# A new instruction order for the first stage of a three-part kernel, and a last output copied by two engines

## The chip, the cores and the metric

The kernel runs on one core of one Trainium2 chip. The metric is device time in microseconds (us) of one execution. The core's engines each run their own instruction stream in order: TensorE does matmuls (PE in the rows), VectorE is DVE, ScalarE is ACT, GpSimd is POOL, and SyncE (SP) issues nearly all DMA transfers.

## The reference, cut to what matters

Three computations follow each other; all of it is in float32.

```python
# attention: q, k, v, f_logit are (4, 8, 768, 48)
f = 1 / (1 + exp(-f_logit))
for t in range(768):
    state = f[:, :, t, :, None] * state + einsum('bhd,bhe->bhde', k[:, :, t], v[:, :, t])
    y[:, :, t] = einsum('bhd,bhde->bhe', q[:, :, t], state)
x = y as (4, 768, 384)
# first block
theta = x @ w_theta                                   # 384 x 384
u = x + w_tok_r @ (x * cos(theta)) + w_tok_i @ (x * sin(theta))   # 768 x 768 each, per batch
x = u + relu(u @ w_ch)                                # 384 x 384
# second block
h = relu(x @ w_in); u, v = h[..., :512], h[..., 512:]
v_n = (v - mean(v)) / sqrt(var(v) + 1e-6)
v_s = w_spatial @ v_n + b_spatial                     # 768 x 768, per batch
out = (u * v_s) @ w_out                               # 512 x 384
```

## The kernel before, in words

**Two stages.** Stage 1 computes attention and the first block for all four batches and prepares the weights of the second block. It ends some 357 to 365 us into the span, the engines not all at the same time. Stage 2 does the second block, one batch after the other, and fills the rest.

**Exact products.** A float32 operand is split into a high and a low part; a product of two split operands is three matmuls. So a row of a group such as `pv` x9 is one output tile: three slices of the contraction, three matmuls each.

**Names in stage 1.** `k`, `q`, `f`, `cw`, `icp`, `cu`, `fs` and `qp` belong to attention: `pt` are transposes of k, `psc` the scores (masked by DVE into `sc`), `pw` the sums of the state (scanned by DVE into `cu`), `px` the attention output, which lands in `X`. `pth` is theta. `acc` is token mixing: `tk` is a slice of the mixing weights, brought by DMA, and `z` is x times cosine or sine. DVE's `xt<-acc,xt` adds the mixing result to x, `uT<-xt,uT` makes its low part, and `hh<-uT,wc` is the product with `w_ch`. DVE's `xt<-hh,xt` adds the relu of that and so frees the PSUM bank of `hh`. `x2d<-xt` stores the result to DRAM. Between these stand the weights of stage 2: `ws`, `wb`, `wi`, `wo` (loaded, split, kept in SBUF) and `X`, `wt`, `wz` with stores `wpd`, which turn `w_spatial` (loaded by `X<-wp_dram` into the buffer `X0` that held a batch of x before) into the blocks of a seven-product scheme.

**Names in stage 2.** Per batch: `pv` (6 tiles of 9 matmuls, 128x512), whose relu ACT writes to `vr`; DVE takes its statistics (`st`, `mv`, small `l` chains, of which ACT does two steps) and normalises it; `pu` (8 tiles of 9); `vn` are the seven operands made from the normalised v by ACT (high part) and DVE (low part); `pg` are seven products of 18 matmuls (P1, P2, P6, P7, P4, P5, P3 in that order) with `sp`, the blocks of `w_spatial` loaded back from DRAM; DVE combines and gates them (`g`, `gt`); `po` (6 tiles of 12) is the product with `w_out`, which ACT copies to `oo` and SP stores to `out_dram`. P1 needs the first three of the six normalised tiles, P2 the other three.

**What sets the order.** In stage 1 it is written out. Every operation is recorded by `Plan` (so all rows carry line L258, the helper's); the operations of a matmul group form one unit, every other operation is a unit of its own, and the table `LINE` (line 65 on) lists the units of each engine in the order in which the engine must run them: "T" TensorE, "V" VectorE, "A" ScalarE, "G" GpSimd, "Q" SyncE. `Plan.run` (lines 233 to 258) chains each engine's instructions accordingly. In stage 2 the tile scheduler orders the instructions by itself, from the order in which `p2_v`, `p2_b`, `p2_u`, `p2_f`, `p2_o` ask for them and from when it thinks operands are there.

**Around the boundary.** Stage 2's PSUM pool has eight buffers on the same eight banks that stage 1 used, so a `pv` tile can start only when the last reader of the bank's old content is done. `flag` (line 1021) runs at the start of stage 2: DVE reduces `ge` to `gt` and `gr`, SP moves `gr` to one partition (`gc<-gr`), DVE sums it (`gs<-gc`), and the result decides at the very end, in a branch (line 1270), whether a general fallback runs. With these inputs it does not run.

**The start.** `run(...)` puts FILL = 16 matmuls of an identity matrix by itself (`pt<-ident`) into the stream. Their result is not used; they keep TensorE busy while the first operands are made.

**The outputs.** `p2_o` (lines 1009 to 1018) takes a tile `oo` from a pool with two buffers, has ACT copy the PSUM tile into it and has SP store it.

## Time and profile before

| | us |
|---|---|
| median of 3 runs | 611.06 |
| lowest, highest | 609.41, 612.85 |
| the profiled execution, its own time | 613.34 |
| span of its trace, first to last instruction | 611.6 |
| TensorE matmul busy | 580.7 (95%) |
| VectorE busy | 454.0 (74%) |
| ScalarE busy | 355.4 (58%) |
| GpSimd busy | 31.9 (5%) |
| mean granted TensorE clock, as a share of full speed | 0.979 |

The profiled execution is 2.28 us longer than the median, and 1.7 us of its time lie outside the span. Times in the trace count from the start of the span. TensorE is busy nearly all the time, so what matters are the few places where it is not, and the few where its granted clock is at the lower of its two levels. How such a row is read: a line of the timeline gives start, duration, engine, operation, output <- inputs, how many instructions are drawn together, and in brackets the idle time of that engine just before and what ended it.

### The profile page before, as it was taken

The numbers are of one execution on the slowest core, as the hardware profiler recorded it, in microseconds if no ns is written. First come the engines' busy times: TensorE is split into PE (matmuls) and PEld (weight loads), VectorE is DVE, ScalarE is ACT, GpSimd is POOL, SyncE is SP. The second block draws the span as 40 slices with busy tenths as digits, with TensorE's granted clock in tenths as the row PEclk, the third lists the DMA queues.
The fourth block names the chain that finished last, engine by engine and source line by source line (L and its number), as shares of the span: only waits on it lengthen the run. The fifth ranks groups of instructions, "written<-read, shape, count | busy, mean of one in ns | idle before, by whom it ended". The sixth has DMA issues, their size and how long they took to land. (4 is left out here: it accounts for less than half of the span.)

```text
span 611.6 us, 14051 instructions
## 1 busy us (share of the span) xinstructions
PE 580.7 (95%) x5686; PEld 532.2 (87%) x5686; DVE 454.0 (74%) x815; ACT 355.4 (58%) x683; POOL 31.9 (5%) x95
## 2 busy tenths in 40 slices
PE   5699999999999999999999959999999999999994
PEld 5676667867989999999999948999999999999994
DVE  4988999888886587776768684896669576948680
ACT  5778897679784798656753252634443444335321
POOL 4410101000110010100000000000000000000000
PEclk9789999999999999999999998999999999999998
DMA  7669768679877897678788979496029504930511
GB/s 238 190 216 332 240 235 276 211 222 308 283 278 277 267 315 254 219 255 266 248 315 309 350 267 302 138 376 243 27 94 379 211 13 140 374 132 1 182 70 65
DMA packets 68442, 139.45 MB, mean 228 GB/s; under 512 B 6480, under 2 KB 40656, under 8 KB 68368
## 3 DMA queue, kind: packets, MB, share of 16 engines
q1 hardware_dynamic: 68368, 138.46, 66.6%
q8 instruction: 47, 0.77, 0.5%
q14 instruction: 27, 0.22, 0.1%
HBM read 104.20 MB, written 31.85 MB: 222 GB/s over the span
## 5 line engine op out<-in xcount | busy, mean ns | idle before, releaser
L258 PE MATMUL acc<-tk,z 128*128 128x384 f32 x792 | 172.2, 367 | 0.4 <-DMA tk<-tkp 0.4
L258 PEld LDWEIGHTS acc<-tk,z 128*128 128x128 f32 x792 | 138.3, 188 | 16.5 <-DMA tk<-tkp 0.7
L258 PE MATMUL pg<-sp,vn 128*128 128x384 f32 x504 | 88.0, 336 | 0.0
L258 PEld LDWEIGHTS pg<-sp,vn 128*128 128x128 f32 x504 | 87.4, 188 | 0.0
L258 PE MATMUL pv<-wi,x 128*128 128x512 f32 x216 | 53.5, 406 | 5.8 <-DVE xt L258 5.8
L258 PEld LDWEIGHTS pv<-wi,x 128*128 128x128 f32 x216 | 42.4, 197 | 15.0 <-DVE xt L258 6.2
L258 PE MATMUL po<-wo,gt 128*128 128x384 f32 x288 | 51.8, 338 | 0.0
L258 PEld LDWEIGHTS po<-wo,gt 128*128 128x128 f32 x288 | 50.8, 188 | 0.3
L258 PE MATMUL pu<-x,wi 128*128 128x384 f32 x288 | 50.7, 334 | 0.0
L258 PEld LDWEIGHTS pu<-x,wi 128*128 128x128 f32 x288 | 50.1, 188 | 0.3
L258 PE MATMUL hh<-uT,wc 128*128 128x384 f32 x216 | 41.7, 342 | 1.1 <-ACT uT L258 0.7
L258 PEld LDWEIGHTS hh<-uT,wc 128*128 128x128 f32 x216 | 37.9, 188 | 2.4 <-ACT uT L258 1.0
L258 ACT ACTIVATE gt<-g 128x384 fp32r<-128x384 f32 x32 | 16.7, 522 | 37.5 <-DVE g L258 37.3
L258 DVE BATCH_NORM_STATS2 st<-vr 128x6 f32<-128x512 f32 x24 | 16.6, 691 | 27.2 <-ACT vr L258 27.1
L258 DVE TENSOR_TENSOR vn<-vr,vn 128x768 fp32r<-128x768 f32 x24 | 22.9, 955 | 18.6 <-ACT vn L258 17.9
L258 ACT ACTIVATE vn<-vr 128x768 fp32r<-128x768 f32 x24 | 20.3, 845 | 20.0 <-PE pg L258 17.9
L258 PE MATMUL pth<-wh,xT 128*128 128x384 f32 x108 | 31.7, 348 | 0.0
L258 PE MATMUL px<-vc,sc 64*64 64x48 f32 x768 | 28.0, 225 | 0.0
L258 ACT ACTIVATE sn<-sn 128x384 f32<-128x384 f32 x48 | 24.9, 520 | 5.1 <-DVE sn L258 4.7
L258 ACT ACTIVATE oo<-po 128x384 f32<-128x384 f32 x24 | 11.8, 492 | 26.1 <-PE po L258 21.3
L258 PEld LDWEIGHTS px<-vc,sc 64*64 64x64 f32 x768 | 25.5, 144 | 0.1
L258 ACT ACTIVATE ws<-ws 128x768 f32<-128x768 f32 (+2 forms) x28 | 20.6, 737 | 6.8 <-DMA ws<-wi_dram 3.3
(138 smaller groups left out, 1053.8 us busy)
## 6 DMA issues: line engine op xcount, KB each, us to landing
sp<-wpd SPq DMA_DIRECT2D x56, 576.0 KB, 6.5
tk<-tkp SPq DMA_DIRECT2D x48, 384.0 KB, 4.9
ws<-tok_dram SPq DMA_DIRECT2D x12, 768.0 KB, 6.0
tkp<-tk SPq DMA_DIRECT2D x24, 384.0 KB, 6.5
tkd<-tk SPq DMA_DIRECT2D x12, 384.0 KB, 5.7
x2d<-xt SPq DMA_DIRECT2D x24, 192.0 KB, 3.8
ws<-tkd SPq DMA_DIRECT2D x12, 384.0 KB, 5.0
xs<-x2d SPq DMA_DIRECT2D x12, 384.0 KB, 6.6
```

Source lines behind the costliest of these rows:

```text
L258: r = f(*a, **k)
```

## The change

All five rows of `LINE` are replaced: the same units on the same engines, in another order. `p2_o` gets a third buffer for `oo` in all batches, and for the very last output tile the PSUM tile is copied in two halves, left by ACT and right by DVE, each stored by a DMA of its own, the left issued by SP and the right by ACT.

```diff
 LINE = {
     "T": [
-        45, 61, 46, 47, 82, 48, 49, 50, 51, 52, 53, 54, 55, 56, 57, 58, 59, 60, 95, 91, 100, 120, 131, 127, 142, 136, 146, 151, 160, 156, 165, 185,
+        45, 61, 46, 47, 48, 49, 50, 51, 52, 53, 54, 55, 56, 57, 58, 59, 60, 82, 91, 95, 100, 120, 127, 131, 136, 142, 146, 151, 156, 160, 165, 185,
...
-    def p2_o(self, out):
+    def p2_o(self, out, last=False):
         gt, wo = self.gt, self.wo
         for t in range(NT):
             sl = slice(P * t, P * t + P)
             p = self.p2.tile([P, FF], F32, name="po", tag="mm")[:, 0:DM]
             self.mm3(p, [(gt[0][:, f, sl], gt[1][:, f, sl], wo[0][:, f], wo[1][:, f]) for f in range(NF)])
-            o = self.d2.tile([P, DM], F32, name="oo", tag="oo")
-            self.A.activation(o, p, AF.Copy)
-            self.Q.dma_start(out=out[sl, :], in_=o)
+            o = self.d2.tile([P, DM], F32, name="oo", tag="oo", bufs=3)
+            if last and t == NT - 1:
+                lo, hi = slice(0, DM // 2), slice(DM // 2, DM)
+                self.A.activation(o[:, lo], p[:, lo], AF.Copy)
+                self.V.tensor_copy(o[:, hi], p[:, hi])
+                self.Q.dma_start(out=out[sl, lo], in_=o[:, lo])
+                self.A.dma_start(out=out[sl, hi], in_=o[:, hi])
+            else:
+                self.A.activation(o, p, AF.Copy)
+                self.Q.dma_start(out=out[sl, :], in_=o)
             yield
...
-            run(self.p2_o(a["out"][b]))
+            run(self.p2_o(a["out"][b], b == B - 1))
```

What the table does shows in the instruction streams. Three places follow; a row is one instruction, or several alike with their count, and a number behind a name tells buffers and operations apart.

VectorE, the last instructions of stage 1, before; `hh_4718` and `hh_4734` are the last two `hh` tiles:

```order
L258 TENSOR_TENSOR X0_134<-X0_134,wz_4698 128x768
L258 TENSOR_SCALAR wb_4820<-ws_4821 128x384
L258 SCALAR_TENSOR_TENSOR wb_4820<-ws_4821,wb_4820 128x384 x2
L258 TENSOR_TENSOR X0_134<-X0_134 128x768
L258 TENSOR_TENSOR wo1_4349<-wb_4820,wo0_4348 128x384
L258 TENSOR_TENSOR wt_4699<-wt_4699,wz_4698 128x384
L258 TENSOR_SCALAR wb_4829<-ws_4830 128x384
L258 TENSOR_TENSOR wt_4699<-wt_4699,X0_134 128x768
L258 SCALAR_TENSOR_TENSOR xt_4067<-hh_4718,xt_4067 128x384
L258 SCALAR_TENSOR_TENSOR wb_4829<-ws_4830,wb_4829 128x384 x2
L258 TENSOR_TENSOR wo1_4349<-wb_4829,wo0_4348 128x384
L258 SCALAR_TENSOR_TENSOR xt_4067<-hh_4734,xt_4067 128x384
```

The reader of `hh_4718` stood behind eight rows of weight work, and that of `hh_4734`, stage 1's last row on this engine, behind two more. The same place in the changed kernel:

```order
L258 TENSOR_TENSOR wo1_4349<-wb_4811,wo0_4348 128x384
L258 TENSOR_SCALAR wb_4820<-ws_4821 128x384
L258 SCALAR_TENSOR_TENSOR xt_4067<-hh_4718,xt_4067 128x384
L258 SCALAR_TENSOR_TENSOR xt_4067<-hh_4734,xt_4067 128x384
L258 SCALAR_TENSOR_TENSOR wb_4820<-ws_4821,wb_4820 128x384 x2
L258 TENSOR_TENSOR X0_134<-X0_134 128x768
L258 TENSOR_TENSOR wo1_4349<-wb_4820,wo0_4348 128x384
L258 TENSOR_TENSOR wt_4699<-X0_134,wt_4699 128x384
L258 TENSOR_TENSOR X0_134<-X0_134,wz_4698 128x768
L258 TENSOR_TENSOR wt_4699<-wt_4699,X0_134 128x768
L258 TENSOR_SCALAR wb_4829<-ws_4830 128x384
L258 SCALAR_TENSOR_TENSOR wb_4829<-ws_4830,wb_4829 128x384 x2
```

The last two readers of `hh` have moved ahead of most of the weight work; nine rows of it now stand behind them before stage 1 ends on this engine (the seven shown and two more, for `wt` and `wo1`).

VectorE, a little earlier, where the last three `acc` tiles are read, before:

```order
L258 TENSOR_TENSOR xt_4067<-acc_4486,xt_4067 128x384
L258 TENSOR_TENSOR uT1_4673<-xt_4067,uT0_4672 128x384
L258 SCALAR_TENSOR_TENSOR xt_3917<-hh_4528,xt_3917 128x384
L258 TENSOR_TENSOR xt_4067<-acc_4488,xt_4067 128x384
L258 TENSOR_TENSOR xt_4067<-acc_4487,xt_4067 128x384
L258 TENSOR_TENSOR uT1_4673<-xt_4067,uT0_4672 128x384 x2
L258 TENSOR_TENSOR wt_4699<-X0_134 128x384
L258 TENSOR_TENSOR X0_134<-X0_134 128x384
```

and in the changed kernel:

```order
L258 TENSOR_TENSOR xt_4067<-acc_4486,xt_4067 128x384
L258 TENSOR_TENSOR wt_4699<-X0_134 128x384
L258 TENSOR_TENSOR X0_134<-X0_134 128x384
L258 TENSOR_TENSOR uT1_4673<-xt_4067,uT0_4672 128x384
L258 TENSOR_TENSOR xt_4067<-acc_4488,xt_4067 128x384
L258 TENSOR_TENSOR xt_4067<-acc_4487,xt_4067 128x384
L258 TENSOR_TENSOR uT1_4673<-xt_4067,uT0_4672 128x384 x2
```

The two operations that read the last load of `w_spatial` into `X0` have moved ahead of the second and third `acc` reader. On SP that load's two transfers stand four and seven rows earlier than before, each still behind the stores that read the buffer's old content.

TensorE at the very start, before; `k0_137` and `k1_203` are the k of the first two attention units:

```order
L258 MATMUL pt_178<-ident_60 128x128
L258 MATMUL pt_195<-ident_60,k0_137 128x128 x3
L258 MATMUL pt_178<-ident_60 128x128 x2
L258 MATMUL pt_223<-ident_60,k1_203 128x128 x3
L258 MATMUL pt_178<-ident_60 128x128 x13
L258 MATMUL pw_252<-vn0_100,kt_110 64x48
```

and in the changed kernel:

```order
L258 MATMUL pt_178<-ident_60 128x128
L258 MATMUL pt_195<-ident_60,k0_137 128x128 x3
L258 MATMUL pt_178<-ident_60 128x128 x15
L258 MATMUL pt_223<-ident_60,k1_203 128x128 x3
L258 MATMUL psc_235<-qp0_105,k0_137 64x64 x12
L258 MATMUL pw_252<-vn0_100,kt_110 64x48
```

Fifteen fillers stand together now, ahead of the second unit's transposes instead of around them, and the first scores stand ahead of the first state sums.

## Rows read from the trace of the kernel before

**Rows 1.** Windows: length, busy us per engine, PEclk, DMA share, GB/s.

```profile
core 0: us, PE busy (x) PEld busy (x) DVE busy (x) ACT busy (x) POOL busy (x), PEclk, DMA share, GB/s
20.00:40.00 20.00, 15.89 (x378) 14.18 (x377) 17.54 (x34) 14.86 (x42) 6.42 (x22) 0.68 0.66 214
140.00:160.00 20.00, 20.00 (x190) 17.83 (x189) 18.63 (x27) 16.94 (x30) 1.21 (x4) 1.00 0.98 340
360.00:380.00 20.00, 15.27 (x57) 12.71 (x58) 9.44 (x30) 5.90 (x13) 0.00 (x0) 0.83 0.86 277
```

**Rows 2.** Chain that ended last, in time order: start, us, what.

```profile
364.74 13.32 PE pv L258 x45
...
390.57 21.84 PE pg L258 x126
...
429.22 8.20 PE pv L258 x36
```

**Rows 3.** Timeline, all engines, end of stage 1.

```profile
356.75 2.24 PE L258 MATMUL pv<-wi,x 128*128 128x512 f32 x9
...
361.46 0.55 DVE L258 SCALAR_TENSOR_TENSOR xt<-hh,xt 128x384 f32<-128x384 f32 x1
...
362.03 2.99 SPq L258 DMA_DIRECT2D x2d<-xt  x3
363.10 0.52 ACT L258 ACTIVATE wo<-wb 128x384 fp32r<-128x384 f32 x1 [2.55 <-DVE wb L258]
...
364.13 0.55 DVE L258 SCALAR_TENSOR_TENSOR xt<-hh,xt 128x384 f32<-128x384 f32 x1
...
364.74 13.32 PE L258 MATMUL pv<-wi,x 128*128 128x512 f32 x45 [5.75 <-DVE xt L258]
```

**Rows 4.** Windows around two pauses of TensorE.

```profile
181.00:184.00 3.00, 1.70 (x38) 1.33 (x36) 1.30 (x2) 2.85 (x5) 0.00 (x0) 1.00 1.02 374
...
364.00:371.00 7.00, 6.26 (x15) 4.96 (x16) 3.18 (x11) 2.61 (x5) 0.00 (x0) 0.52 0.69 195
```

**Rows 5.** Timeline, the flag and the operands of the first products.

```profile
369.63 0.61 SPq L258 DMA_DIRECT2D gc<-gr  x1
...
376.39 0.27 DVE L258 TENSOR_REDUCE gs<-gc 1x1 f32<-1x128 f32 x1 [8.14 <-DMA gc<-gr]
376.59 0.67 DVE L258 BATCH_NORM_STATS2 st<-vr 128x6 f32<-128x512 f32 x1
...
383.37 0.93 DVE L258 TENSOR_TENSOR vn<-vr,vn 128x768 fp32r<-128x768 f32 x1
...
388.60 0.96 DVE L258 TENSOR_TENSOR vn<-vr,vn 128x768 fp32r<-128x768 f32 x1
```

**Rows 6.** Timeline, the last load of `w_spatial` and the last `acc` readers.

```profile
345.65 0.81 SPq L258 DMA_DIRECT2D X<-wp_dram  x2
...
347.19 0.56 DVE L258 TENSOR_TENSOR xt<-acc,xt 128x384 f32<-128x384 f32 x1 [1.45 <-PE acc L258]
...
352.91 0.56 DVE L258 TENSOR_TENSOR wt<-X 128x384 f32<-128x384 f32 x1 [0.88 <-DMA X<-wp_dram]
```

**Rows 7.** Timeline, the fillers and the first scores.

```profile
6.44 0.90 PE L258 MATMUL pt<-ident,k 128*128 128x128 f32 x3 [3.47 <-DVE k L258]
...
10.02 4.19 PE L258 MATMUL pt<-ident 128*128 128x128 f32 x26
...
14.52 0.88 PE L258 MATMUL psc<-qp,k 64*64 64x64 f32 x24
...
15.52 0.56 DVE L258 TENSOR_TENSOR sc<-psc,mask 128x384 f32<-128x384 f32 x1 [3.18 <-PE psc L258]
```

**Rows 8.** Timeline, the last outputs.

```profile
598.75 4.39 PE L258 MATMUL po<-wo,gt 128*128 128x384 f32 x24
...
601.27 3.49 SPq L258 DMA_DIRECT2D out_dram<-oo  x3
...
603.92 0.49 ACT L258 ACTIVATE oo<-po 128x384 f32<-128x384 f32 x1 [1.43 <-DMA out_dram<-oo]
```

122 rows, old and new, of the table LINE are left out of this document.

## The prediction

> **What bounds the kernel now.** I read the share of busy time first: TensorE's matmuls are busy 95% of the span, so time is won only where TensorE waits, where it runs at its lower clock, or behind its last matmul. The 20 us windows then show where that is. From 44 to 340 us every window is full; [rows 1] shows one of the fullest for all engines, 140 to 160, with VectorE at 18.63 of 20. Two places are not full. From 20 to 40 TensorE is busy 15.89 at a mean clock of 0.68, and from 360 to 380 it is busy 15.27 at 0.83 [rows 1].
>
> The chain that ended last gives the second place its parts [rows 2]: `pv` 13.32 us, `pu` up to 390.57, `pg` 21.84. The timeline shows what lies ahead [rows 3]: the first `pv` tile starts at 356.75 and ends at 358.99, then TensorE stands still for 5.75 us until 364.74, and the row names VectorE's `xt`. That is the reader of the last `hh` tile, at 364.13, which frees a PSUM bank; the reader before it runs at 361.46. Their own inputs did not hold them: TensorE runs in order, so the matmuls of `hh` were over about when `pv` began at 356.75. VectorE was working through weights.
>
> The pause has a second price. In the window behind it the granted clock is 0.52, that is the lower level (1.2 of 2.4 GHz) for nearly all of it [rows 4]. The 45 `pv` matmuls took 13.32 us; the next batch's 36 took 8.20, 0.228 each, by which 45 take 10.25 [rows 2]. So 3.07 us went to the clock. A shorter pause did not do that: TensorE is busy only 1.70 of 3.00 us from 181 to 184, around a pause of 1.3, and the clock stays 1.00 [rows 4].
>
> **The change part by part.** *End of stage 1.* The two last readers of `hh` now stand ahead of nine rows of weight work. VectorE can run them as soon as `hh` is done, some 357.5 us, ahead of 358.99 when the second `pv` tile wants its bank. So TensorE goes on at 358.99, without the pause and the lower clock: `pv` ends at 358.99 + 10.25 = 369.24, `pu` (390.57 - 378.06 = 12.51) at 381.75. If nothing else were late, `pg` would start 8.82 us earlier, and all of stage 2 behind it. ScalarE does not spoil this: its last work of stage 1 still waits for VectorE's weights to about 363.6 [rows 3], but the pool has eight buffers for six `pv` tiles, so its copies are wanted only when the third `pu` tile comes, after 372.
>
> What is late next is the operands of `pg`. VectorE needs the normalised `v`, and in its stream stands the flag's sum `gs`, which waits for a transfer: issued at 369.63, there at 376.39, VectorE idle 8.14 us for it [rows 5]. Behind it, P2's operand `vn` ends at 388.60 + 0.96 = 389.56, 13.17 after `gs` began. The changed kernel has four BN_STATS ahead of `gs` where before had one: 3 x 0.67 = 2.0 less behind it. The first tile's small chain and normalising now stand behind it: one tile of the five that took the 13.17, so at most 2. I take 12.5 (11.2 to 13.2). The transfer itself is behind the stores on SP. Before, the three stores of the last `xt` held SP 2.99 us until 365.0 [rows 3]; now these go out some 6 us earlier, but the last stores of weights still wait for VectorE, whose total work is the same. I take the flag as landing 2.0 earlier, at 374.4, between no gain (376.4) and the 2.4 that the rest of the 2.99 could give. Then P2's operand is there at 386.9. Its products and all behind, 108 of 126 matmuls, take 18.72, so `pg` ends at 405.6 instead of 412.41: **6.8 us gained**. Bounds: with the flag as before and 13.2 behind it, P2 is ready at 389.6 and the gain is 4.1; with nothing late it is 8.8. P1's operand (383.37 before, 5.2 us ahead of P2's) comes at about 382, so TensorE waits twice for about a microsecond; by the pause of 1.3 in [rows 4] I let the clock stay up.
>
> By the Trainium skill (TensorE: Matmul & The Clock Gate, "What's actually happening") the throttled state is the default and activity releases it; the 0.52 behind the 5.75 us pause agrees. The 1.00 around the pause of 1.3 agrees too, and what the rule would make of two pauses close together is the first rival.
>
> *Start.* Before, the first scores `psc` stood behind 13 fillers (26 records, 10.02 to 14.21) and began at 14.52, and VectorE idled 3.18 us for them [rows 7]. Now 15 fillers follow directly on the first unit's transposes (which begin at 6.44); at 0.32 each they end at about 12, then three transposes of 0.5 in sum, and `psc` may begin at 12.4, about 2.1 earlier. VectorE's own row, added up to the first `z` product with the traced durations, is 2.3 shorter. These are the same gain seen from two engines, so I take **2.0** for the whole start. How much of it arrives at 44 us is uncertain, since TensorE's clock is at the lower level in a third of this stretch (0.68, [rows 1]): bounds -2 (the clock falls in other places) and +5 (psc, VectorE's row and a better clock all count).
>
> *Middle, 44 to 340 us.* TensorE is full and the same matmuls run: 0. Moved weight and store work is covered by TensorE's own work; that cover is thinnest at 140 to 160, where VectorE is at 18.63 of 20. Bounds -4 and +1.
>
> *Tail.* The last `oo` copy waited for a buffer, 1.43 us after the one before and until the store issued at 601.27 had landed [rows 8]; the last matmul ends at 598.75 + 4.39 = 603.14. With three buffers it starts about 0.7 earlier than 603.92, and half a tile takes about half of 0.49: **0.9** (0.5 to 1.0). That the halves go out on two engines saves one issue on SP at most; the span ends 611.6, long behind either.
>
> The Trainium skill (DMA: Bandwidth & Descriptors, "Issuing engines are not separate DMA queues") says that issuing from two engines saves only the issuing time, which speaks against a gain from the split store. No row here has one. The sum does without it: it rests on the copy.
>
> *Sum.* 6.8 + 2.0 + 0 + 0.9 = 9.7. The profiled execution goes from 613.34 to 603.6; it lies 2.28 above the median, and the same difference on 611.06 gives **601.4**. Own range: with end and start both at their good bounds it would be 5.0 less, at their bad ones 6.7 more; two thirds of these give 598.1 to 605.9.
>
> **The rivals.** *The flag takes most of it back.* If the flag lands as before, the gain there is 4.1. TensorE then waits about 1.5 for P1 and 2 for P2; if that lowers the clock, another 3.07 goes. 4.1 - 3.07 = 1.0, and 1.0 + 2.0 + 0.9 = 3.9, so 607.2. For it: the last weight stores ahead of the flag wait for the same VectorE work as before. Against it: P1's 18 matmuls lie between the two pauses.
>
> *A new wait on a load, and the kernel is slower.* VectorE now reads the last load of `w_spatial` ahead of the second and third `acc` readers. It gets there at 347.19 + 0.56 = 347.75. Before, the load was issued at 345.65 and used only at 352.91, after waiting 0.88 for it [rows 6]. Each microsecond that it lands after 347.75 holds up `uT`, `hh` and stage 2, and beyond about 2 the clock's 3.07 comes on top. Landing at 352.9 as before costs 5.2 + 3.07 = 8.3, so 609.7 and almost nothing gained. It decides against the change from 354.3 on (9.7 - 3.07 = 6.6 past 347.75), and by 358 the kernel is at 614.7. For it: the load's buffer must first be stored, and the store waits for VectorE. Against it: the transfers stand four and seven rows earlier on SP; at 345.65 less about 0.5 us a row they go at 342 to 343 and land by 349, a loss of about one us that the third `acc` reader, which waits for TensorE anyway, mostly hides.
>
> *VectorE becomes the bound in the middle, or the start gains nothing.* VectorE's work ahead of the `acc` reader near 144 us grows by 2.7 by the same adding up, against a slack of 1.37 in the window [rows 1]. If that and a start of 0 come together, 6.8 + 0.9 - 1.3 to -4 = 3.7 to 6.4: 604.7 to 607.4, about 606.
>
> *The order does not do what it says.* If another reader still holds the second `pv` tile's bank, only the start and the tail remain: 2.9, 608.2.
>
> **How the numbers follow.** Forecast 0.56 (598.1 to 605.9); better than that 0.06; flag 0.13 (607.2); load 0.10, of which half beyond 354.3; middle or start 0.11 (606); no release 0.04 (608.2). A measurement of this kernel can tell about 0.5%, 3.06 us, from no change: faster means below 608.0, slower above 614.1. Faster: 0.56 + 0.06 + 0.12 of the flag + 0.01 of the load + 0.10 of the middle + 0.01 = 0.86. Same 0.10, most of it the load between 350 and 354 and past it a little. Slower 0.04. The range leaves out the load's worse half, the best tenth of the start and the cases without release: 596.5 to 608.5.
>
> **What would show it.** Right: no pause between the first `pv` tile and the next over 0.3 us, a clock of 1.00 from 356 to 380, `pv` over by 367 to 371 (the start's gain included), `pg` over by about 404, and `psc` beginning at 12 to 13. Wrong: VectorE idle ahead of `wt<-X` with a DMA as releaser near 348; `gs` later than 375; a clock below 1 in 380 to 390; TensorE waiting for VectorE between 130 and 150; or the last `oo` copy still released by a DMA.

## The result, and the profile after

| | before | after |
|---|---|---|
| median, both kernels measured on the same chip, us | 611.95 | 601.82 |
| lowest, highest | 609.41, 614.19 | 599.95, 603.56 |
| ratio, 95% interval | | 0.984 (0.980 to 0.987) |
| the profiled execution, its own time | 613.34 | 599.95 |
| span of its trace | 611.6 | 598.2 |

The changed kernel is faster by 10.1 us; 601.4 was forecast. The two profiled executions differ by more, 13.4 us: that of before lies 1.4 above its median, that of after is the fastest of its kernel, 1.9 below its median. Pieces read from these two traces therefore add up to 13.4, and not to 10.1.

Windows of the kernel after, with the columns of [rows 1] (stretch, length, busy us of each engine, granted clock, DMA share, GB/s), the three stretches shown there and three more:

```profile
20.00:40.00 20.00, 16.90 (x395) 14.71 (x386) 17.01 (x35) 15.14 (x41) 6.36 (x22) 0.74 0.73 236
...
140.00:160.00 20.00, 20.00 (x227) 18.21 (x227) 18.96 (x27) 17.53 (x28) 1.41 (x5) 1.00 0.97 352
360.00:380.00 20.00, 20.00 (x111) 19.18 (x110) 14.73 (x52) 12.32 (x30) 0.00 (x0) 1.00 0.94 307
380.00:400.00 20.00, 20.00 (x117) 20.00 (x116) 18.58 (x32) 8.48 (x13) 0.00 (x0) 1.00 0.94 325
400.00:420.00 20.00, 18.20 (x96) 16.78 (x95) 11.14 (x27) 6.91 (x15) 0.00 (x0) 1.00 0.57 208
...
180.00:200.00 20.00, 20.00 (x365) 18.97 (x363) 14.72 (x22) 14.55 (x26) 1.55 (x5) 1.00 0.93 330
```

From 360 to 380 TensorE is busy all 20 us at a clock of 1.00, where it had 15.27 at 0.83 [rows 1]. The start is a little fuller (16.90 for 15.89, clock 0.74 for 0.68). A new gap stands from 400 to 420: 18.20. And from 180 to 200 TensorE is full, where before had 18.70 at a clock of 1.00.

The end of stage 1, timeline of all engines, which answers [rows 3] and [rows 6]:

```profile
343.65 0.55 DVE L258 TENSOR_TENSOR wt<-X 128x384 f32<-128x384 f32 x1
...
351.93 1.20 DVE L258 SCALAR_TENSOR_TENSOR xt<-hh,xt 128x384 f32<-128x384 f32 x2
352.38 12.44 PE L258 MATMUL pv<-wi,x 128*128 128x512 f32 x54
```

All 54 `pv` matmuls run in one piece; the two readers of `hh` end at 353.13, before the second tile wants its bank (354.45). The read of the last load of `w_spatial` at 343.65 waits for nothing. The rest of [rows 2] in the chain of waits of after (start, us, what):

```profile
352.54 12.28 PE pv L258 x54
364.82 12.51 PE pu L258 x72
...
417.55 8.65 PE pv L258 x38
```

The flag and the operands, which answer [rows 5], all engines:

```profile
362.75 0.62 SPq L258 DMA_DIRECT2D gc<-gr  x1
...
368.86 0.27 DVE L258 TENSOR_REDUCE gs<-gc 1x1 f32<-1x128 f32 x1 [1.65 <-DMA gc<-gr]
...
374.44 0.95 DVE L258 TENSOR_TENSOR vn<-vr,vn 128x768 fp32r<-128x768 f32 x1
377.16 22.00 PE L258 MATMUL pg<-sp,vn 128*128 128x384 f32 x126
378.62 0.96 DVE L258 TENSOR_TENSOR vn<-vr,vn 128x768 fp32r<-128x768 f32 x1
```

`pg` waits for no operand at all: P1's is there at 375.4, P2's at 379.58, and P2 begins about 380.3, after P1's 18 matmuls. What came late instead lies further on, ahead of the fourth `po` tile of the first batch. A tile's twelve matmuls come in two groups of six, and this is the seventh group, as it is called below:

```profile
391.26 0.33 SPq L258 DMA_DIRECT2D xs<-x2d  x1
...
397.62 0.85 ACT L258 ACTIVATE x<-xs 128x768 fp32r<-128x768 f32 x1 [6.70 <-DMA xs<-x2d]
398.38 0.93 ACT L258 ACTIVATE gt<-g 128x384 fp32r<-128x384 f32 x2
...
407.30 1.32 PE L258 MATMUL po<-wo,gt 128*128 128x384 f32 x6 [1.80 <-ACT gt L258]
```

The start and the last outputs, which answer [rows 7] and [rows 8]:

```profile
7.00 5.03 PE L258 MATMUL pt<-ident 128*128 128x128 f32 x30
...
12.29 0.86 PE L258 MATMUL psc<-qp,k 64*64 64x64 f32 x22
...
13.25 0.56 DVE L258 TENSOR_TENSOR sc<-psc,mask 128x384 f32<-128x384 f32 x1 [1.28 <-PE psc L258]
```

```profile
592.03 0.33 ACT L258 ACTIVATE oo<-po 128x192 f32<-128x192 f32 x1 [0.74 <-PE po L258]
592.39 0.36 DVE L258 COPY oo<-po 128x192 f32<-128x192 f32 x1 [7.11 <-ACT oo L258]
```

The last copy no longer waits for a store; but VectorE's half runs behind ScalarE's, not beside it.

Two tables, worked out from the matmul records, carry what follows. First landmarks (us; the start of the matmul, if nothing else is said), each row one profiled execution:

| kernel | last `acc` | first `pv` | second `pv` tile | first `pu` | second batch's `pu` | last matmul ends | span |
|---|---|---|---|---|---|---|---|
| before | 349.94 | 356.75 | 364.74 | 377.90 | 437.26 | 603.14 | 611.6 |
| after | 345.92 | 352.38 | 354.45 | 364.65 | 426.04 | 591.95 | 598.2 |
| e1_table | 344.45 | 350.92 | 352.98 | 363.18 | 424.51 | 590.89 | 598.1 |
| e2_out | 351.18 | 357.46 | 365.13 | 378.14 | 437.50 | 603.40 | 611.7 |
| e4_readers | 349.29 | 355.57 | 357.63 | 367.83 | 427.50 | 593.40 | 601.8 |
| e3_behind | 346.30 | 352.76 | 360.72 | 372.97 | 432.33 | 598.32 | 604.4 |
| e9_bank | 351.39 | 359.29 | 361.35 | 371.55 | 436.79 | 602.70 | 611.5 |
| h1_start | 350.52 | 357.31 | 362.63 | 374.58 | 434.66 | 600.73 | 607.4 |
| h2_end | 359.88 | 366.35 | 368.43 | 378.63 | 439.51 | 605.42 | 612.5 |
| e8_fill | 347.98 | 355.22 | 363.29 | 375.57 | 434.93 | 600.84 | 609.9 |
| e10_xlast | 345.54 | 352.00 | 354.08 | 364.28 | 427.22 | 593.61 | 600.0 |
| e11_xsoon | 345.91 | 352.37 | 354.43 | 364.63 | 425.22 | 591.12 | 597.3 |

Second, when TensorE had the same work behind it. At the six places of this table all five kernels have started the same number of matmuls of every kind, so that times in one row can be compared; each is the start of the next matmul (us).

| matmuls started | before | e2_out | e8_fill | after | e1_table |
|---|---|---|---|---|---|
| 786 | 54.16 | 54.16 | 51.80 | 50.34 | 49.05 |
| 1396 | 95.48 | 95.66 | 94.00 | 91.88 | 90.57 |
| 1579 | 101.69 | 101.87 | 100.26 | 99.29 | 98.39 |
| 2391 | 178.89 | 179.26 | 177.38 | 176.99 | 175.51 |
| 2696 | 190.28 | 192.19 | 188.96 | 186.85 | 185.38 |
| 4258 | 331.80 | 333.04 | 329.84 | 327.77 | 326.31 |

before and e2_out run the old table, after and e1_table the new one, so the two pairs (before and after, e2_out and e1_table) say how far a difference repeats. before and e2_out run stage 1 alike and still lie 1.9 us apart after 2,696 matmuls; a difference of that size between two single executions need not be one between their kernels.

### The profile page after: what moved, and what is told of

It reads as the page before. It is cut to its first block, busy times and chain, and to the rows that moved or that the text cites. A ratio compares the mean times of both kernels' runs of the same rounds, so it can differ in the third digit from the quotient of the medians.

```text
span 598.2 us, 14051 instructions
## 1 busy us (share of the span) xinstructions
PE 575.8 (96%) x5686; PEld 529.2 (88%) x5686; DVE 452.7 (76%) x816; ACT 355.4 (59%) x683; POOL 30.7 (5%) x95
## 4 chain that ended last, share of the span: by engine, by line
PE 89%; DVE 4%; DMA 2%; ACT 1%; issue 1%; DVEq 0%; ACTq 0%
PE acc L258 27%; PE pg L258 11%; PE pu L258 8%; PE pv L258 8%; PE po L258 7%; PE pth L258 7%; PE hh L258 6%; PE px L258 4%; PE psc L258 4%; PE pt L258 3%; PE pw L258 3%; DVE g L258 1%; DMA xs<-x2d 1%; DMA ws<-tok_dram 1%; DVE vn L258 1%
## 5 line engine op out<-in xcount | busy, mean ns | idle before, releaser
L258 PE MATMUL acc<-tk,z 128*128 128x384 f32 x792 | 171.2, 368 | 0.0
L258 PEld LDWEIGHTS acc<-tk,z 128*128 128x128 f32 x792 | 138.7, 189 | 16.2 <-issue 0.5
L258 PE MATMUL pg<-sp,vn 128*128 128x384 f32 x504 | 88.0, 336 | 0.0
L258 PEld LDWEIGHTS pg<-sp,vn 128*128 128x128 f32 x504 | 87.4, 188 | 0.0
L258 PE MATMUL po<-wo,gt 128*128 128x384 f32 x288 | 52.1, 338 | 1.8 <-ACT gt L258 1.8
L258 PEld LDWEIGHTS po<-wo,gt 128*128 128x128 f32 x288 | 50.8, 188 | 2.4 <-ACT gt L258 2.1
L258 PE MATMUL pu<-x,wi 128*128 128x384 f32 x288 | 50.7, 335 | 0.0
L258 PEld LDWEIGHTS pu<-x,wi 128*128 128x128 f32 x288 | 50.1, 188 | 0.3
L258 PE MATMUL pv<-wi,x 128*128 128x512 f32 x216 | 50.4, 390 | 0.0
L258 PEld LDWEIGHTS pv<-wi,x 128*128 128x128 f32 x216 | 40.5, 188 | 8.1
L258 PE MATMUL hh<-uT,wc 128*128 128x384 f32 x216 | 42.0, 343 | 0.8 <-ACT uT L258 0.7
L258 PEld LDWEIGHTS hh<-uT,wc 128*128 128x128 f32 x216 | 37.7, 188 | 1.9 <-ACT uT L258 1.0
L258 DVE BATCH_NORM_STATS2 st<-vr 128x6 f32<-128x512 f32 x24 | 16.5, 690 | 26.5 <-ACT vr L258 26.5
L258 DVE TENSOR_TENSOR vn<-vr,vn 128x768 fp32r<-128x768 f32 x24 | 22.9, 954 | 17.3 <-ACT vn L258 16.5
L258 ACT ACTIVATE gt<-g 128x384 fp32r<-128x384 f32 x32 | 16.5, 521 | 32.0 <-DVE g L258 31.9
L258 PE MATMUL pth<-wh,xT 128*128 128x384 f32 x108 | 32.1, 351 | 0.0
L258 ACT ACTIVATE vn<-vr 128x768 fp32r<-128x768 f32 x24 | 20.3, 844 | 18.2 <-PE pg L258 17.3
L258 PE MATMUL px<-vc,sc 64*64 64x48 f32 x768 | 27.8, 223 | 0.0
L258 ACT ACTIVATE ws<-ws 128x768 f32<-128x768 f32 (+2 forms) x28 | 20.4, 732 | 11.0 <-DMA ws<-wo_dram 5.1
L258 ACT ACTIVATE u<-pu 128x384 f32<-128x384 f32 x32 | 15.7, 490 | 18.5 <-PE pu L258 18.5
L258 ACT ACTIVATE sn<-sn 128x384 f32<-128x384 f32 x48 | 24.9, 520 | 2.2 <-DVE sn L258 1.7
L258 PEld LDWEIGHTS px<-vc,sc 64*64 64x64 f32 x768 | 25.4, 143 | 0.0
```

Source lines behind the costliest of these rows:

```text
L258: r = f(*a, **k)
```

## The experiments

Each ratio is to the kernel before, measured beside it. Where a table takes more lines, the helper's rows carry L265 instead of L258.

**e1_table and e2_out: the two halves of the change apart.** e1_table has the new table and `p2_o` of before; e2_out the old table and the new `p2_o`.

```diff
 e1_table, against after
-            o = self.d2.tile([P, DM], F32, name="oo", tag="oo", bufs=3)
-            if last and t == NT - 1:
...
+            o = self.d2.tile([P, DM], F32, name="oo", tag="oo")
+            self.A.activation(o, p, AF.Copy)
+            self.Q.dma_start(out=out[sl, :], in_=o)
```

> The new order table with the old outputs (two buffers, last tile in one piece). Theory: the table carries nearly everything; the outputs are worth only the wait for the buffer, so against the kernel before it is 9 us faster (ratio about 0.985), the last output copy waits again about 0.7 us for a store, and the stretch from the last matmul to the end of the span is 8.4 us as before. Rival: the profile of the changed kernel has 6.3 us behind its last matmul against 8.5 before; if the outputs really save these 2.2, this kernel is only about 8 us faster (0.987).

> The old order table with the new outputs (three buffers, last tile in two halves). Theory: 0.9 us faster than before, ratio 0.9985, from the wait for the buffer alone, since the copy of the right half stands behind the copy of the left one in the changed kernel's trace (592.39 after 592.36). Rival: 2.2 us faster (0.9964), the stretch behind the last matmul 6.3 us instead of 8.5, because the program's closing branch comes in one piece.

Measured: e1_table 600.21 us, ratio 0.982 (0.978 to 0.987); e2_out 612.20, ratio 0.999 (0.997 to 1.002). The table is the change. The outputs are worth at most 0.3% of 612, 1.8 us, and the middle of that interval is 0.4. In the traces the last copy ends 1.27 us after the last matmul in before and 0.82 in e2_out; 1.64 in e1_table and 0.80 in after. From the last matmul to the end of the span e1_table takes 7.2 us where 8.4 were expected: a pause of SP, described at the end, is missing there.

**h1_start and h2_end: the two ends of the table apart.** h1_start takes the new order for the first 44 us or so and the old one behind it; h2_end the old order to about 332 us and the new one behind that. At each seam the units that one order had run already, and the other not, were put in the order of the table that follows.

```diff
 h1_start, "T", against before
-        45, 61, 46, 47, 82, 48, 49,
+        45, 61, 46, 47, 48, 49,
...
 h2_end, "V", against before
-        1602, 1603, 1604, 1571, 1606, 1583, 1609, 1579, 1521, 1610, 1611, 1613, 1528,
+        1602, 1521, 1528, 1603, 1604, 1571, 1606, 1569, 1575, 1579, 1609, 1610, 1611, 1583, 1613,
```

> The old kernel with the new order for the first 285 units of stage 1 (about the first 44 us) and the old order behind them. Theory: the start is worth 2.0 us (ratio 0.9967): the first scores at about 12.3 instead of 14.5, the first acc some 2 to 4 us earlier. Rival: the start gains nothing that lasts, because TensorE has the same waits for the scans a few us earlier and the lower clock in another place; then 0 and the ratio 1.000. The pause of 5.75 us near 360 stays in both.

> The old kernel with the old order up to about 332 us and the new order for the last 132 units of stage 1. Theory: the end alone carries most of the gain, 6.8 us (ratio 0.989): no pause in pv, clock 1.00 from 356 to 380, and 8.8 us gained at the start of pg, of which TensorE gives about 2 back waiting for the gated operands of po in the first batch. Rival: the end is worth all of 8.8 or more and the start and the middle nothing; or only about 5, if the gain of the changed kernel comes as much from the middle.

Measured: h1_start 607.88, ratio 0.993 (0.990 to 0.995); h2_end 614.09, ratio 1.003 (1.001 to 1.006). Neither total can be taken at its face. In h1_start the last `acc` came no earlier than before (350.52). With the same matmuls behind it TensorE was 1.9 us ahead at 24 us and 1.0 ahead at 49, behind the seam, where it waited 2.29 us for `cu` (46.76). It kept this 1.0 to 186 us and lost 1.5 in the next 4 us, where the granted clock fell behind a pause (0.91 from 180 to 200, more on this below). Its gain came behind that: at the boundary, where the pause was shorter, and in the 1.8 us less from the last matmul to the end of the span (6.65, before 8.49). TensorE's timeline:

```profile
357.31 2.22 PE L265 MATMUL pv<-wi,x 128*128 128x512 f32 x9
362.63 3.68 PE L265 MATMUL pv<-wi,x 128*128 128x512 f32 x8 [3.10 <-DVE xt L265]
```

The new start had shifted which `hh` tile lay in which PSUM bank: the second `pv` tile got the bank of the last tile but one, whose reader ran at 362.02, and not that of the last, read at 364.70. In h2_end the seam set TensorE back by 6.72 us, waiting for a slice of mixing weights:

```profile
335.12 5.05 PE L265 MATMUL acc<-tk,z 128*128 128x384 f32 x20 [6.72 <-DMA tk<-tkp]
```

Behind the seam `pv` runs in one piece from 366.35, 12.44 us, and from the last `acc` to the second batch's `pu` 79.6 us pass, before 87.3; the end of the new table carries these 7.7. A table spliced from two orders tests the seam first; the following experiments move single units.

**e4_readers: the old kernel with two units moved.** The two last readers of `hh` stand right behind the product of `X0` with `wz`; nothing else is changed.

```diff
 "V", against before
-        1575, 1602, 1603, 1604, 1571, 1606, 1583, 1609, 1579, 1521, 1610, 1611, 1613, 1528,
+        1575, 1521, 1528, 1602, 1603, 1604, 1571, 1606, 1583, 1609, 1579, 1610, 1611, 1613,
```

> The old kernel with one edit to its table: on VectorE the readers of hh_4718 and hh_4734 stand right behind the X0 product at 356 us instead of behind eight and ten rows of weight work. Theory: these two rows are the whole pause, so it goes (under 0.5 us instead of 5.75), the clock stays 1.00 from 356 to 380, pu starts 8 to 9 us earlier than 378, the first batch gives 1.5 to 2.5 back ahead of its last po tiles, and the time falls by 6 to 7 (ratio about 0.989). Rival: it was the late flag and the weights behind it that mattered, and with only two rows moved pg waits for its operands: 2 to 4 us gained (0.995).

Measured: 603.81, ratio 0.986 (0.982 to 0.990), 8.6 us. TensorE's timeline and the window behind it:

```profile
355.57 12.43 PE L265 MATMUL pv<-wi,x 128*128 128x512 f32 x54
367.83 12.67 PE L265 MATMUL pu<-x,wi 128*128 128x384 f32 x72
...
360.00:380.00 20.00, 20.00 (x107) 18.64 (x106) 13.69 (x50) 10.88 (x28) 0.00 (x0) 1.00 1.03 335
```

No pause, a clock of 1.00. From the last `acc` to the first `pu` 18.54 us pass, before 27.96: 9.4 less. And next to nothing is given back, where 1.5 to 2.5 were expected: from `pu` to the next batch's `pu` 59.67, before 59.36.

**e3_behind: the changed kernel with the two units put back** behind the weights.

```diff
 "V", against after
-        1568, 1599, 1602, 1521, 1528, 1603, 1604, 1571, 1606, 1569, 1575, 1579, 1609, 1610, 1611, 1583, 1613,
+        1568, 1599, 1602, 1603, 1604, 1571, 1606, 1569, 1575, 1579, 1609, 1521, 1610, 1611, 1583, 1613, 1528,
```

> The changed kernel with those two readers put back behind the weight work (the first ahead of the last three rows of stage 1, the second as the last). Theory: the pause of 5 to 6 us and the lower clock behind it come back, and of the 10 us that the change gained about 6.7 are lost: ratio to the kernel before 0.994. Rival: the order ahead of it leaves VectorE so much earlier that the pause is 2 us or less and the ratio stays below 0.988.

Measured: 605.23, ratio 0.988 (0.984 to 0.992). The pause and the lower clock are back, timeline and window:

```profile
360.72 12.42 PE L265 MATMUL pv<-wi,x 128*128 128x512 f32 x45 [5.73 <-DVE xt L265]
...
360.00:380.00 20.00, 19.28 (x86) 16.95 (x87) 10.45 (x38) 7.74 (x20) 0.00 (x0) 0.88 0.89 289
```

The first `pu` comes 26.67 us after the last `acc`, in after 18.73. The second batch's `pu`, however, is only 6.3 us later than in after, because the 1.8 us wait of `po` is gone with it (59.36 from `pu` to `pu`, in after 61.39). By its time the kernel loses less than expected (0.994): 0.988 against 0.984, and the two intervals overlap. That it stays 7 us faster than before fits its trace, in which it keeps 3.6 at the last `acc` and 2.4 behind the last matmul.

**e9_bank: the old kernel with other banks.** Is it the bank that holds TensorE up, or the late readers as such? Two tiles of one column are taken from the PSUM pool in the first batch, so that the tiles behind them lie in other banks, and no early `pv` tile lies in the bank of a late `hh`. VectorE's order is that of before.

```diff
 p2_v, against before
+        first = not getattr(self, "begun", False)
+        self.begun = True
...
+            if first and s == 1:
+                for _ in range(2):
+                    V.memset(self.p2.tile([P, FF], F32, name="skip", tag="mm")[:, 0:1], 0.0)
```

> The old kernel and table, but the second to sixth pv tiles of the first batch go to PSUM banks 5, 4, 1, 2 and 3 instead of 7, 6, 5, 4 and 1 (two tiles are taken ahead of them, each with a memset of one column by VectorE). Banks 7 and 6 held the last two hh tiles. Theory: TensorE waited not for VectorE's work as such but for bank 7; with other banks pv runs through without a pause although the readers are as late as before, and pu starts 8 to 9 us earlier; the time falls by 5 to 7 (0.990). Rival: the second pv tile needs something else that VectorE makes at 364, for example a weight, and the pause stays at 5 us or more (1.000).

Measured: 611.28, ratio 0.998 (0.995 to 1.001): at most 0.5% won. Timeline of all engines:

```profile
359.29 12.43 PE L258 MATMUL pv<-wi,x 128*128 128x512 f32 x54
...
367.05 0.55 DVE L258 SCALAR_TENSOR_TENSOR xt<-hh,xt 128x384 f32<-128x384 f32 x1
367.86 0.60 ACT L258 ACTIVATE vr<-pv 128x512 f32<-128x512 f32 x1
...
377.58 0.27 DVE L258 TENSOR_REDUCE gs<-gc 1x1 f32<-1x128 f32 x1 [6.40 <-DMA gc<-gr]
...
379.53 6.83 PE L258 MATMUL pu<-x,wi 128*128 128x384 f32 x36 [1.55 <-ACT vr L258]
...
390.80 18.66 PE L258 MATMUL pg<-sp,vn 128*128 128x384 f32 x106 [0.37 <-DVE vn L258]
```

The pause in `pv` is gone and TensorE reaches `pu` 6.35 us earlier than in before. But the last reader still runs at 367.05, so the last stores, the flag (377.58) and the operands come as late as ever; TensorE waits 1.33 for `xt`, 1.55 for `vr`, 0.32 and 0.37 for `vn` and 2.2 for `gt`, and the second batch's `pu` begins at 436.79, before 437.26. Counted from the last `acc`, 1.9 us are won up to there (85.4, before 87.3), in an execution in which VectorE also waited 1.96 us for the last load of `w_spatial`, before 0.88 [rows 6]. The theory held for the pause and fell for the time: the bank was where the lateness showed, and most of the price lies in the lateness itself.

**e8_fill: the old kernel with the fillers in one piece.** One unit of "T", the second k's transposes, goes behind the last filler.

```diff
 "T", against before
-        45, 61, 46, 47, 82, 48, 49, 50, 51, 52, 53, 54, 55, 56, 57, 58, 59, 60, 95,
+        45, 61, 46, 47, 48, 49, 50, 51, 52, 53, 54, 55, 56, 57, 58, 59, 60, 82, 95,
```

> The old kernel with one number of its table moved: the transposes of the second unit's k stand behind all fillers instead of between them, so 15 fillers run together from about 7 us. Theory of the prediction: the first scores start 2 us earlier (12.5 instead of 14.5) and this is most of the start's gain, 1 to 2 us at the first acc (52.4 before) and 0.998 of the time. Rival: the fillers are not what the start waits for, because the scans behind the scores come no earlier; the first acc stays within 0.5 us of 52.4 and the time is the same.

Measured: 609.41, ratio 0.995 (0.993 to 0.997). TensorE's timeline:

```profile
7.04 4.48 PE L265 MATMUL pt<-ident 128*128 128x128 f32 x30
...
13.34 0.86 PE L265 MATMUL psc<-qp,k 64*64 64x64 f32 x22 [1.00 <-ACT qp L265]
```

The scores begin at 13.34, before at 14.52, and 12.5 was expected. With the same matmuls behind it TensorE is 2.4 us ahead of before after 786 of them, 1.3 after 2,696 and 2.0 after 4,258, and the last `acc` comes 2.0 earlier. So this one unit carries some 2 us of the start.

**Where the 2 us ahead of `po` come from: e6_flag, e10_xlast, e11_xsoon.** In after, `po` waits 1.80 us for ScalarE's `gt`, which runs behind ScalarE's `x<-xs`, which waits 6.70 us for a load. Three changed kernels, each with one cause taken away: the flag's steps asked for only behind the first batch's `p2_f`; VectorE's third `x<-xs` of the first batch placed behind the last product of the gates; the first `x<-xs`, on VectorE and on ScalarE, no longer ordered behind the last `vn`, so that its buffer is free for the third load earlier. The expectation of the last speaks of VectorE alone; the edit frees both, and ScalarE's copy moved from 387.99 to 376.33.

```diff
 e6_flag
-        self.flag(self.d1, bad)
...
             run(self.p2_f(f))
+            if b == 0:
+                self.flag(self.d1, bad)
 e10_xlast, in p2_x
+            if j == NJ - 1 and not self.plan.on and not getattr(self, "late", False):
+                self.late = True
+                self.tc.add_manual_dep(y.ins, self.gated, mybir.DependencyInfo(mybir.DependencyClass.NoSync, mybir.DependencyReason.DATA), reason="order")
...
-        V.tensor_tensor(g, g, self.u2[:, f, tl], op=ALU.mult)
+        self.gated = V.tensor_tensor(g, g, self.u2[:, f, tl], op=ALU.mult).ins.name
 e11_xsoon, in p2_x
+            if j == 0 and not self.plan.on and not getattr(self, "soon", False):
+                self.soon = True
+                continue
             for i, z in zip((x, y), self.end):
```

> The changed kernel with the flag's instructions asked for behind the products of the first batch, so that its sum stands behind P2's operand on VectorE instead of ahead of the first normalising. Theory: VectorE is the engine that is late in the first batch, by the flag's wait (1.65 us) and sum; without it the wait of 1.8 us ahead of the seventh po group goes, and the kernel is 1.5 to 2 us faster than the changed one (ratio to the kernel before about 0.980). Rival: the load of the next batch's x, which ScalarE and VectorE wait for at 397 us, sets that time; then the wait stays at 1.5 us or more and the ratio at 0.983 to 0.984.

> The changed kernel with one order constraint more: in the first batch VectorE's third x<-xs stands behind the last gate product g<-g,u instead of ahead of the last four gated tiles. Theory: the wait of 1.8 us ahead of the seventh po group is that operation, 0.96 us long and 0.94 us late by its load; without it the wait goes and the first batch takes 59.4 to 59.8 us from pu to pu instead of 61.4, the kernel 1.5 to 2 us faster than the changed one (ratio to the kernel before about 0.980). Rival: VectorE's work for the gates in pairs is what is late; the wait falls by less than half, or comes back ahead of pv, which needs that x.

> The changed kernel, with one dependency dropped: VectorE's first x<-xs of the first batch no longer has to come behind the last vn, so it stands ahead of P2's vn instead of behind it. In the changed kernel this copy ran at 390.28 us; its xs buffer was loaded anew from 391.26 us, 6.3 us; ScalarE's x<-xs waited 6.70 us for that load until 397.62, its gt came behind it, and TensorE's po waited 1.8 us for gt (407.30). If this chain of loads is the cause of the po wait: the copy runs before about 380 us, the third load is issued some 10 us earlier, ScalarE's 6.7 us wait for xs falls below 2, the po wait is under 0.5 us, the first batch from pu to pu takes 59.4 to 60.0 us (61.4 before), and the time is 1.5 to 2 us below the changed kernel's (ratio to the kernel before about 0.980). If instead the paired gate products themselves are too slow for po, the po wait stays at 1.5 or more with ScalarE not waiting for xs. If the 0.96 us copy now ahead of P2's vn is what counts, TensorE waits up to 1 us at the first pg on P2 and nothing is won.

Measured: e6_flag 600.53, ratio 0.982 (0.979 to 0.985); e10_xlast 599.81, 0.978 (0.975 to 0.982); e11_xsoon 600.15, 0.980 (0.977 to 0.983). By their intervals none can be told from the changed kernel's 0.984 (0.980 to 0.987) with any certainty; the traces tell them apart. First e6_flag, then e10_xlast (timeline and a window), then e11_xsoon, all engines:

```profile
407.00 1.32 PE L258 MATMUL po<-wo,gt 128*128 128x384 f32 x6 [1.61 <-ACT gt L258]
```

```profile
397.66 0.85 ACT L258 ACTIVATE x<-xs 128x768 fp32r<-128x768 f32 x1 [7.11 <-DMA xs<-x2d]
...
398.95 1.03 DVE L258 TENSOR_TENSOR gt<-g,gt 128x384 fp32r<-128x384 f32 x2 [1.75 <-ACT gt L258]
...
406.88 1.79 PE L258 MATMUL po<-wo,gt 128*128 128x384 f32 x6 [1.75 <-ACT gt L258]
...
400.00:420.00 20.00, 18.25 (x89) 16.72 (x88) 11.85 (x31) 6.70 (x16) 0.00 (x0) 0.91 0.54 195
```

```profile
377.47 0.95 DVE L258 TENSOR_TENSOR x<-xs,x 128x768 fp32r<-128x768 f32 x1
378.45 0.33 SPq L258 DMA_DIRECT2D xs<-x2d  x1
...
397.58 1.00 ACT L258 ACTIVATE gt<-g 128x384 fp32r<-128x384 f32 x2 [6.42 <-DVE g L258]
...
406.47 1.32 PE L258 MATMUL po<-wo,gt 128*128 128x384 f32 x6 [0.99 <-ACT gt L258]
```

Taking the flag out of VectorE's stream changes next to nothing ahead of `po` (1.61 for 1.80); that theory fell. e10_xlast's fell too: with its own copy out of the way, VectorE waits 1.75 us for ScalarE's `gt`, which stands behind the copy that waits for the load. From `pu` to `pu` it even takes 62.94, after 61.39, because behind this wait its clock was lower (0.91 from 400 to 420, in after 1.00). With the load early in e11_xsoon, ScalarE never waits for `xs` there, and the wait of `po` falls to 0.99, from `pu` to `pu` to 60.59 (after 61.39, before 59.36). So half of the first expectation holds: the load is about half of the wait. What is left is the other expectation: ScalarE now waits 6.42 us for VectorE's gate products, which VectorE does without a gap. That VectorE's work lies in a shorter stretch than before (busy 14.73 of 20 us from 360 to 380, before 9.44 [rows 1]) does not explain it alone: in e4_readers it is 13.69, and `po` hardly waits. What differs is the order. `po` waits for the seventh of the eight `gt` that ScalarE makes: in after, e11_xsoon and e4_readers the group starts 0.05 to 0.06 us behind its end. ScalarE's last two, first e4_readers, then e11_xsoon:

```profile
408.13 0.53 ACT L265 ACTIVATE gt<-g 128x384 fp32r<-128x384 f32 x1 [1.03 <-DVE g L265]
409.19 0.53 ACT L265 ACTIVATE gt<-g 128x384 fp32r<-128x384 f32 x1 [0.54 <-DVE g L265]
```

```profile
405.90 0.93 ACT L258 ACTIVATE gt<-g 128x384 fp32r<-128x384 f32 x2
```

In e4_readers VectorE finishes one gate and then the next, and the two end 6.5 and 7.5 us behind the start of `po`. In after and e11_xsoon it does two gates in turn, step by step, and in e11_xsoon they end 7.4 and 7.9 behind it: the eighth 0.3 later than in e4_readers, the seventh 1.0, about the wait that is left. This order is the scheduler's, and no run changed it alone.

**e7_three: the changed kernel with three buffers and the last tile in one piece.**

```diff
 p2_o, against after
-            if last and t == NT - 1:
-                lo, hi = slice(0, DM // 2), slice(DM // 2, DM)
...
+            self.A.activation(o, p, AF.Copy)
+            self.Q.dma_start(out=out[sl, :], in_=o)
```

> The changed kernel with the third buffer for the outputs but the last tile in one piece. Theory: the third buffer is the whole gain at the end and the halves add nothing, since the right half's copy started only after the left one's: the last copy starts 0.1 us behind the last matmul, and from the last matmul to the end of the span it takes 6.0 to 6.6 us as in the changed kernel (6.3). Rival: the halves save their 0.2 us or more, so that this kernel needs 6.6 to 7.

Measured, in two runs: 600.12, ratio 0.980 (0.976 to 0.984), not to be told from the changed kernel. The last copy, ScalarE's timeline:

```profile
591.42 0.49 ACT L258 ACTIVATE oo<-po 128x384 f32<-128x384 f32 x1 [0.74 <-PE po L258]
```

It ends 0.57 us after the last matmul (591.34), in after 0.80, and the span ends 6.45 after it, as expected. The third buffer does it; the halves cost 0.2 at this point, because the second runs behind the first.

## Why the prediction was right, and where

The time, 601.4 forecast and 601.82 measured, is right as a sum of terms of which two were too small (the start and the middle), one right for another reason (the end of stage 1), and one blind to part of what it stood for (the tail). In traces the gain is 13.4 us where the sum said 9.7. That the medians differ by 10.1, so close to the sum, is therefore in part luck.

**The release at the end of stage 1: 8.82 gross forecast, 8.2 to 9.2 measured.** From the last `acc` to the first `pu` before and e2_out take 27.96 and 26.96 us, after and e1_table 18.73 and 18.73. e4_readers shows it alone (9.4), e3_behind its loss (26.67). Both parts are as worked out: the pause of 5.75 is gone, and the clock of 360 to 380 is 1.00. (Ten rows of weight work stand behind the two readers now, not nine: eight are shown ahead of the prediction, and two follow.)

**What is given back: 2.0 forecast, 2.0 measured, in another place.** The step that failed is the flag. It was put at 374.4 and P2's operand 12.5 behind it at 386.9, with `pg` waiting. Measured, `gs` ran at 368.86 and the operand was there 10.7 later, below the least that was allowed for (11.2); `pg` did not wait. Stage 1 ended 4.0 us earlier, and of the 7.5 by which `gs` came earlier 3.5 are the flag's own, for which 2.0 was taken and 2.4 was the bound. Its transfer was issued 2.9 sooner behind the last `acc` than in before (16.8 us for 19.7) and took 6.1 us for 6.8. What was late next stood one step further: the gates, ahead of the seventh `po` group, from `pu` to `pu` 61.39 for 59.36. The prediction followed the chain only to `pg`. The net of 6.8 is met by 7.2 and 6.3 (from the last `acc` to the second batch's `pu`, the two pairs), so the agreement of this term is partly luck. e4_readers, with the same release and VectorE's old order behind it, gives nearly nothing back, and h2_end, with the new order's end alone, 1.5 (60.88 from `pu` to `pu`): the 2.0 go with the new order, not with the release. About half of them is the late load, as e11_xsoon shows; the rest goes with the order of the gates, which is read from traces and was not changed by itself.

**The start: 2.0 forecast, 3.8 and 5.1 measured** after 786 matmuls, at about 50 us. `psc` begins at 12.29, as said (12.4). e8_fill shows 2.4 of it to be the one moved unit. The term was sized from one row, and the wait ahead of the first scores is not all of what the new start saves.

**The middle: 0 forecast, 0.2 and 1.6 measured,** the rest of larger parts. From 786 to 2,391 matmuls, up to about 179 us, the new order loses 1.9 and 1.3 against the old one; 1.2 and 1.6 go between 1,396 and 1,579, where it has a new wait, of 1.40 us for `X` at 97.11 in after. From there to 2,696, at about 190, it wins 1.5 and 3.1: there the old order has the pause that [rows 4] show, and e2_out a lower clock behind it. The prediction read every window from 44 to 340 as full. That of the pause was not, 18.70 of 20 (first row below), although the pause was quoted for another purpose, and three others lacked 0.4 to 0.5. Start and middle together came to 4.0 and 6.7 where 2.0 were forecast.

**The clock at short pauses: not reliable as told.** From [rows 4] it was read that a pause of 1.3 us leaves the clock up. In e2_out the same pause (1.31 us, at 183.0), at the same place of the same order, goes with a lower one; windows of before, then of e2_out:

```profile
180.00:200.00 20.00, 18.70 (x383) 17.56 (x376) 11.74 (x18) 11.60 (x21) 0.21 (x1) 1.00 0.81 285
180.00:200.00 20.00, 18.69 (x399) 17.54 (x390) 11.90 (x17) 10.45 (x19) 0.21 (x1) 0.91 0.79 284
```

It is 0.91 also in h1_start and e9_bank, and 1.00 also in h2_end. The price can be read from e2_out: at 186 us it is 0.4 behind before, with the same matmuls done, and 3 us later 1.9, so 1.5 went to the clock. The waits ahead of the seventh `po` group differ in the same way: 1.75 us with a lower clock behind it in e10_xlast, 1.80 without one in after. [Rows 4] gave one execution's answer. The forecast let the clock stay up over two pauses of this kind ahead of `pg`; they did not occur, so the error cost nothing.

**The tail: 0.9 forecast.** The copy that waited for a store starts right behind the last matmul, as said; it ends 0.45 earlier in the pair with the old table and 0.84 in that with the new one. The halves add nothing (e7_three). Not foreseen was a pause of SP behind the outputs, below, which makes 1.85 of the 2.2 us by which the profiled executions differ behind the last matmul.

**The rivals.** The load of `w_spatial` was there in time. The flag took nothing back. VectorE did not become the bound from 140 to 160 (TensorE 20.00 of 20). The order did what it says; h1_start shows, though, that which `hh` tile lies in the wanted bank does change with the start of the table, and that 2.7 us hang on it where the readers are late (a pause of 3.10 for 5.75).

**Open.** The pause near 183 us, released by "issue" (the profile shows nothing that TensorE waited for), occurs in before, e2_out, h1_start, h2_end and e9_bank, and in e8_fill as 1.50 us at 186.2, but not in e4_readers, which has the same order there as before. Why is not settled. Not tried: the new table with VectorE's end of stage 1 from e4_readers, which, if the pieces add, would keep the start and give nothing back at `po`.

## What to carry to other kernels

Look past the first operand that a released stage needs: a gain at a boundary can be given back where the engine whose work was merely moved together is next waited for, and that may be two products further on; that it need not be, e4_readers shows. A wait for a buffer names the place where lateness shows; freeing the buffer alone (e9_bank) won at most 0.5%, and moving the late work itself (e4_readers, two instructions) won 8.6 us. And when an ordered list is tested in parts, move single units in one or the other order, since a splice of two orders pays for its seam.

## What the runs showed of the hardware that was not expected

**A pause behind the last output that goes with the length of SP's program.** Behind its last transfer SP branches and runs through a closing row of semaphore instructions, 2.5 to 3.3 us passing to the first of them. In before, e2_out, e4_readers, e8_fill and e9_bank a second pause of 1.85 to 1.98 us follows after the first few; in the other nine traces, after among them, it is not there (the longest at that place is 0.65, in e10_xlast). SP has 667 or 668 instructions in the first five and 670 to 684 in the others. The page's row of instruction packets (queue, packets, MB, share) fits: 27 or 28 in the five, 25 or 26 in the others. Before, then after:

```profile
q14 instruction: 27, 0.22, 0.1%
```

```profile
q14 instruction: 26, 0.21, 0.1%
```

That SP waits there for its next instructions is the obvious reading, and no run tested it. If it is so, some 1.9 us of the gain come from the new program being a few instructions longer on SP.

**Two engines on one tile.** VectorE's copy of the right half of the last tile started when ScalarE's copy of the left half was over, in every trace with halves (7.10 and 7.11 us of idle time, ended by ScalarE's `oo`). Whether the program or the chip puts them one behind the other, no run asked. By the Trainium skill (DMA: Bandwidth & Descriptors, "Issuing engines are not separate DMA queues") a second issuing engine saves only the time of issuing; e2_out agrees, with a ratio of 0.999 (0.997 to 1.002) for all of the change to the outputs.
